# A fused attention and MoE kernel: single token tiles at the start of the first layer, a held weight load, and paired fifth tiles

## The chip, the core and the metric

The kernel runs on one core of one Trainium2 chip. The metric is the device time of one execution in microseconds; the median of the runs is what counts. PE is the matmul engine, PEld its weight loads, DVE the vector engine, ACT the scalar engine, POOL the engine that issues the weight transfers, and SP the queue that issues most other transfers. Each engine works through its own instructions in a fixed order.

## The reference: linear attention, then two matrix products with a gate between them

For 8 batches, 8 heads, 576 tokens and a head size of 64 the reference computes

```
phi(x)  = concat(relu(x) * cos(pos), relu(x) * sin(pos))     # 64 -> 128
kv      = phi(k)^T v          z = sum over tokens of phi(k)  # per batch and head
attn    = phi(q) kv / (phi(q) z + 1e-6)
x       = attn, heads side by side                           # 4608 tokens x 512
h       = x @ w_in                                           # 512 -> 2048
out     = (h * cos(h)) @ w_out                               # 2048 -> 512
```

The inputs q, k, v, w_in and w_out and the output are float32.

## The kernel before

**Tiles.** The 576 tokens of a batch lie on 128 partitions: even and odd partitions hold two blocks of 64 rows. One block has five tokens for each partition and the other four, so a batch has four full token tiles of 128 and a fifth tile in which only 64 rows, every other one, are its own. Which block has the five alternates with the batch. The fifth tiles of two batches fill one tile of 128 tokens, so there are nine groups of 512 tokens for the two layers: `c` = 0 to 7 are the four full tiles of batch `c`, and `c` = 8 collects the fifth tiles of all batches (`xR`).

**Attention of a batch.** `load` (L332) issues the transfers of q, k and v on SP, two for each (four and five tokens for each partition). `prep` (L355) makes relu times cos or sin of one token tile on ACT or DVE, `cast_v` (L369) casts v, and `kv` (L383) multiplies: 40 matmuls of 65 columns, the 65th being a column of ones that gives z. Its result is copied to `kvz`. `q_pe` (L414) transposes a q tile with 8 matmuls and a copy; later batches use a transposing transfer instead (`q_dma`). `num` (L435) multiplies a q tile with `kvz`, 8 matmuls of 65 columns; DVE and ACT then make `den`, `rec` and `x`; `x_pe` (L489) transposes x into `xT`, and `x_dma` does it with a transfer.

**Fifth tiles before.** Each batch has its own prep and transpose of its fifth q tile, into `qT4[b % 2]`. With an odd batch, `num` multiplies both, `parts` of two matmuls accumulating in one bank: the rows that are not a batch's own are zeros there. For that, `first_attention` clears the fifth place of the raw q, k and v on DVE (L962), and cs has zeros in those rows. For batch 0 the fifth q tile is prepared in `late_q0` (L1039), behind the first gate of layer 1, and the one of batches 0 and 1 goes through `num` in `second_attention` (L987).

**Layer 1 and layer 2.** `layer1` (L522) of the first two groups goes by quarters of w_in; each step is 8 matmuls of 256 columns (two token tiles, two blocks of 128 of the 2048 columns) into one of three banks `M1`, followed by `gate` (L511): ACT makes the cosine (as a sine) into `ch`, and DVE multiplies. `layer2_plain` (L771) does layer 2 of group 0 with 512 columns in the two banks `M2`. Later groups use products of sums of blocks (seven products in place of eight), for which `w_in_sums` (L615) writes sums of weights into tiles `WS0` to `WS2`.

**The start.** PE runs filler matmuls (`warm`, L913) until q has landed. POOL issues the weight transfers in `weights` (L920): a small copy waits until k has landed, then come all four quarters of w_in, then w_out's first two quarters behind a copy that waits for w_in's first. `hold_raw` (L945) holds the transfers of batch 1 on a small copy that reads w_in's first quarter.

**Order.** All steps are added to a `Plan` (L142) with their reads and writes. A table of numbers at the top, `KEYS` (L17), one for each step, gives the place of each step in the order, and for steps that can go to several engines which engine does it. Every engine's queue is that order, so it is written out once for the whole kernel.

Of the kernel before, what the change touches and what calls it, by code (L numbers as in the profile page):

```python
# [12 lines left out]
F32 = mybir.dt.float32  # L13
# [180 lines left out]
def kernel(  # L194
# [9 lines left out]
    nc = tc.nc  # L204
# [127 lines left out]
    def load(b, nm, due, hs=(slice(0, H),)):  # L332
        m, n = raw[nm], b % 2
        for h in hs:
# [3 lines left out]
            def go5(h=h, five=five):  # L338
                nc.sync.dma_start(out=blocks(m, n)[:, h], in_=five)
# [711 lines left out]
    for c in range(2, NC):  # L1051
        if c < B:
            attention(c)
# [40 lines left out]
```

## Time and profile before

| what | value |
|---|---|
| median of 3 runs | 281.59 us (280.68 to 282.78) |
| the profiled execution, its own time | 280.85 us |
| its span, first to last instruction | 279.0 us |
| PE busy, PEld, DVE, ACT | 269.2, 217.3, 251.4, 218.9 us |
| mean granted TensorE clock | 0.999 |
| read from HBM, written to it | 36.74 MB, 9.44 MB |
| transposing transfers qT<-KQ after 59 us, time from issue to landing | 29, median 5.1 us |
| matmuls of `num` (L450) | 320 |

The lines of the trace name an engine, a line of the kernel, an operation, and what it writes and reads. Times in the timeline are from the start of the span. A group's mean is the duration of one instruction, and matmuls overlap, so the distance between the starts of two matmuls is shorter than the duration: 16 matmuls of `num` with a mean of 193 ns each take 0.48 us. `MEMSET`, `COPY` and `CAST` are DVE's or POOL's; `LDWEIGHTS` is a weight load of 128 by 128, one ahead of each matmul.

### The profile page before, as it was taken

The numbers are of one execution on the slowest core, as the hardware profiler recorded it, in microseconds if no ns is written. First come the engines' busy times: TensorE is split into PE (matmuls) and PEld (weight loads), VectorE is DVE, ScalarE is ACT, GpSimd is POOL, SyncE is SP. The second block draws the span as 40 slices with busy tenths as digits, with TensorE's granted clock in tenths as the row PEclk, the third lists the DMA queues.
The fourth block names the chain that finished last, engine by engine and source line by source line (L and its number), as shares of the span: only waits on it lengthen the run. The fifth ranks groups of instructions, "written<-read, shape, count | busy, mean of one in ns | idle before, by whom it ended". The sixth has DMA issues, their size and how long they took to land.

```text
span 279.0 us, 6853 instructions
## 1 busy us (share of the span) xinstructions
PE 269.2 (96%) x2715; PEld 217.3 (78%) x2715; DVE 251.4 (90%) x449; ACT 218.9 (78%) x401; POOL 8.3 (3%) x21
## 2 busy tenths in 40 slices
PE   7779999999999999999999999999999999999994
PEld 2458767678766677789879887998788888888883
DVE  2977798999999999999999999999999999998872
ACT  2856698899999999999999999984684686777210
POOL 1430020000000000000000000000000000000000
PEclk9999999999999999999999999999999999999999
DMA  6999999999999999999999999737210400200324
GB/s 208 315 201 232 281 312 282 309 218 172 328 269 253 210 288 247 310 235 230 245 264 195 346 277 265 154 58 205 39 39 4 188 2 0 78 0 2 151 78 150
DMA packets 77599, 53.30 MB, mean 191 GB/s; under 512 B 46080, under 2 KB 75264, under 8 KB 77568
## 3 DMA queue, kind: packets, MB, share of 16 engines
q1 hardware_dynamic: 72608, 48.12, 67.7%
q0 software_dynamic: 4224, 4.19, 9.3%
q10 hardware_dynamic: 736, 0.57, 0.6%
q8 instruction: 21, 0.34, 0.5%
q14 instruction: 10, 0.08, 0.1%
HBM read 36.74 MB, written 9.44 MB: 166 GB/s over the span
## 4 chain that ended last, share of the span: by engine, by line
PE 85%; DMA 5%; ACT 4%; DVE 3%; issue 2%; ACTq 0%
PE M L849 33%; PE M L685 15%; PE M L542 8%; PE M L582 7%; PE TR L685 6%; PE M L784 4%; PE ATT L450 3%; DMA qT<-KQ 3%; PE ATT L391 3%; DMA qm<-in_q_dram 2%; ACT KQ L364 2%; PE TR L582 1%; ACT ch L514 1%; PE M L420 1%; DVE KQ L365 1%
## 5 line engine op out<-in xcount | busy, mean ns | idle before, releaser
L514 ACT ACTIVATE ch<-M 128x512 f32<-128x512 f32 x90 | 53.9, 603 | 14.0 <-PE M L685 6.8
L849 PEld LDWEIGHTS <-gT 128*128 128x128 f16 x560 | 54.1, 98 | 8.2
L519 DVE TENSOR_TENSOR gT<-M,ch 128x512 f16<-128x512 f32 x84 | 55.9, 685 | 4.5 <-ACT ch L514 4.0
L849 PE MATMUL M<-w_out_sb,gT 128*128 128x256 f16 x448 | 56.4, 273 | 0.0
L364 ACT ACTIVATE KQ<-km,CS 128x512 f16<-128x512 f32 x56 | 38.9, 732 | 0.5 <-DMA km<-in_k_dram 0.5
L364 ACT ACTIVATE KQ<-qm,CS 128x512 f16<-128x512 f32 x48 | 33.5, 728 | 4.4 <-DMA qm<-in_q_dram 4.2
L685 PEld LDWEIGHTS <-w_in_sb 128*128 128x128 f16 x320 | 31.0, 98 | 4.6 <-issue 0.2
L849 PE MATMUL M<-T,S 128*128 128x256 f16 x256 | 31.5, 273 | 0.0
L318 ACT ACTIVATE ost<-M 128x512 f32<-128x512 f32 x32 | 19.2, 600 | 15.0 <-PE M L849 9.5
L542 PE MATMUL M<-xT,w_in_sb 128*128 128x256 f16 x256 | 30.1, 272 | 0.6 <-DVE gT L519 0.5
L542 PEld LDWEIGHTS <-w_in_sb 128*128 128x128 f16 x256 | 24.6, 98 | 4.8 <-issue 1.2
L582 PE MATMUL M<-xT,w_in_sb 128*128 128x512 f16 x112 | 27.9, 379 | 0.0
L849 PEld LDWEIGHTS <-S 128*128 128x128 f16 x256 | 24.9, 98 | 3.4
L476 DVE TENSOR_TENSOR x<-ATT,rec 128x512 f16<-128x512 f32 x32 | 22.1, 692 | 2.5
L685 PEld LDWEIGHTS <-WS 128*128 128x128 f16 x216 | 20.6, 98 | 2.6
L582 PEld LDWEIGHTS <-w_in_sb 128*128 128x128 f16 x128 | 11.9, 98 | 9.2
L365 DVE TENSOR_SCALAR KQ<-qm,CS 128x512 f16<-128x512 f32 x32 | 14.2, 479 | 4.8 <-DMA qm<-in_q_dram 4.8
L450 PEld LDWEIGHTS <-qT 128*128 128x128 f16 x320 | 14.7, 98 | 4.4 <-issue 1.4
L323 DVE TENSOR_TENSOR S<-gT 128x2048 f16<-128x2048 f16 (+1 forms) x16 | 17.2, 1083 | 0.0
L450 PE MATMUL ATT<-kvz,qT 128*128 128x65 f16 x288 | 15.3, 194 | 0.9 <-DVE kvz L406 0.4
L323 DVE TENSOR_TENSOR gT<-Z,ch 128x1024 f16<-128x1024 f32 x13 | 15.9, 1219 | 0.3
L698 DVE TENSOR_TENSOR Z<-M,Z 128x512 f32<-128x512 f32 x22 | 14.9, 686 | 0.9 <-PE M L685 0.5
(138 smaller groups left out, 448.6 us busy)
## 6 DMA issues: line engine op xcount, KB each, us to landing
out_dram<-ost SPq DMA_DIRECT2D x33, 256.0 KB, 2.7
qm<-in_q_dram SPq DMA_DIRECT2D x8, 640.0 KB, 5.7
km<-in_k_dram SPq DMA_DIRECT2D x8, 640.0 KB, 6.5
qm<-in_q_dram SPq DMA_DIRECT2D x8, 512.0 KB, 6.0
km<-in_k_dram SPq DMA_DIRECT2D x8, 512.0 KB, 6.5
vm<-in_v_dram SPq DMA_DIRECT2D x6, 640.0 KB, 6.8
vm<-in_v_dram SPq DMA_DIRECT2D x6, 512.0 KB, 6.6
w_in_sb<-in_moe_w_in_dram POOLq DMA_DIRECT2D x4, 512.0 KB, 8.6
```

The source lines that it names most:

```text
L318: "ACT": lambda: nc.scalar.activation(out=out_, in_=in_, func=AF.Copy),
L323: return lambda: q.tensor_tensor(out=out_, in0=in0, in1=in1, op=op)
L364: fn = {"ACT": lambda: nc.scalar.activation(out=out_, in_=in_, func=AF.Relu, scale=sc), "DVE": lambda: nc.vector.tensor_scalar(out=out_, i ...
L365: "DVE": lambda: nc.vector.tensor_scalar(out=out_, in0=in_, scalar1=0.0, scalar2=sc, op0=ALU.max, op1=ALU.mult)}
L450: nc.tensor.matmul(bank[hb][:, hh * D1:(hh + 1) * D1], lhsT=a[:, h, :], rhs=z[:, h, :], start=(i == 0), stop=(i == len(parts) - 1))
L476: nc.vector.tensor_tensor(out=split(x16[n][:, hs, :], k), in0=A[:, :, :, 0:D], in1=split(rec[n][:, hs], k).unsqueeze(3).broadcast_to((P, k ...
L514: act(0.5, due, lambda: nc.scalar.activation(out=ch[c], in_=bank, func=AF.Sin, bias=math.pi / 2.0, scale=1.0), [key], [("ch", c)])
L519: dve(0.61, due, lambda: nc.vector.tensor_tensor(out=dst, in0=a, in1=b, op=ALU.mult), [key, ("ch", c), *rd], dkeys)
L542: nc.tensor.matmul(M1[m][:, jj * 2 * P:(jj + 1) * 2 * P], lhsT=w_in_sb[:, cc, j * P:(j + 1) * P], rhs=X[:, cc, ts], start=(jj == 0 and cc ...
L582: nc.tensor.matmul(M, lhsT=w_in_sb[:, cc, j * P:(j + 1) * P], rhs=X[:, cc, :], start=(cc == 0), stop=(cc == NCT - 1))
L685: nc.tensor.matmul(bank[0][:, j * TH:(j + 1) * TH], lhsT=a(cc, j), rhs=b[:, cc, :], start=(first and j == 0 and cc == 0), stop=(last and j ...
L849: nc.tensor.matmul(bank[0][:, tt * MH:(tt + 1) * MH], lhsT=a[:, j, tt * P:(tt + 1) * P], rhs=b[:, j, :], start=(first and (apart or tt == ...
```

## The change

Three things change, and with them the whole table `KEYS`, so that the order and the engines of many other steps differ too (1,407 steps before, 1,396 after).

*First layer of batch 0.* Quarter 0 of w_in is done by `first_tile`: one token tile at a time, 16 matmuls of 128 columns into one bank. Quarters 1 to 3 stay at 256 columns. The banks of this layer are six, the three `M1`, `TR` and the two `M2`, in place of three. In PE's order the four single tiles stand like this: tile 0, the transposes of x of tiles 3 and 2, then a second tile, a third, one step of 256 columns, and the last tile.

*w_in's second half.* `weights` issues two quarters; `more_weights` issues the other two behind a copy that reads the last V cast of batch 0, and then w_out as before. In POOL's order the hold for q of batch 1 and then the one for k now stand behind w_out's first and second quarter.

*Fifth tiles of q.* The fifth place of the raw q is filled by both batches of a pair, each in its own rows, and is prepared and transposed once, with the odd batch, into one tile `qT4`. Only `num` separates them: for each head two matmuls with 64 weight columns each, every second column of `qT4`, one for the even batch and one for the odd, into rows 0 to 63 and 64 to 127 of the bank. cs gets a sixth column with the fifth tile's factors for all rows. The fifth rows of `xR` are then the even batch's 64 followed by the odd one's, and the stores of group 8 read neighbouring rows. For batches 0 and 1, q is loaded without its fifth token, q's memset is gone, and `first_fifth_tile` loads, prepares and multiplies the fifth tokens later, in the part of group 2; their `kvz` are kept until then in the tile `WS2`, whose weight sums therefore come behind that `num`. `late_q0` is gone.

```diff
     def load(b, nm, due, hs=(slice(0, H),)):
...
-                nc.sync.dma_start(out=blocks(m, n)[:, h], in_=five)
+                nc.sync.dma_start(out=blocks(m, n)[:, h, 0:n5, :], in_=five[:, :, 0:n5, :])
...
+            n5 = NT if b < 2 and nm == "q" else NT + 1
...
+    def load_q5(b, due):
+        five = tokens(src["q"][b])[0]
+        pl.add("SP", 0.65, 0, due, lambda: nc.sync.dma_start(
+            out=blocks(Q5, b), in_=five[:, :, NT, :]),
+            [], [("q5", b), ("Z3", 0, 0)], dma=(R * H * D * 4 / 1e3, 150.0, 55), late=0.9, lazy=LAZY)
...
     def num(b, t, due, pair=None):
...
-        parts = [(qdst(b, t)[0], kvz[b % 2])]
...
-            parts.insert(0, (qT4[1 - b % 2], kvz[1 - b % 2]))
...
-                for i, (a, z) in enumerate(parts):
+                for n2 in range(2) if t == NT else [None]:
+                    rows_, cols, z = (slice(0, P), slice(0, P), kvb(b)[0]) if n2 is None else (
+                        slice(n2 * R, (n2 + 1) * R), slice(n2, P, 2), kvb(b - 1 + n2)[0])
                     nc.tensor.matmul(
-                        bank[hb][:, hh * D1:(hh + 1) * D1], lhsT=a[:, h, :], rhs=z[:, h, :],
-                        start=(i == 0), stop=(i == len(parts) - 1))
+                        bank[hb][rows_, hh * D1:(hh + 1) * D1], lhsT=a[:, h, cols], rhs=z[:, h, :],
+                        start=True, stop=True)
...
+    def first_tile(X, xk, G, t):
+        ring = BANKS + BANKS2
+        M, mk = ring[m1n[0] % len(ring)]
+        m1n[0] += 1
+        due = start[0] + t * width[0] / NJT
+        ts = slice(t * P, (t + 1) * P)
+
+        def mm():
+            for j in range(4):
+                for cc in range(NCT):
+                    nc.tensor.matmul(
+                        M[:, j * P:(j + 1) * P], lhsT=w_in_sb[:, cc, j * P:(j + 1) * P], rhs=X[:, cc, ts],
+                        start=(j == 0 and cc == 0), stop=(j == 3 and cc == NCT - 1),
+                        skip_group_check=True)
+        full[mk] = True
+        pe(4 * NCT, MMT, due, mm, xk[t:t + 1] + [("w_in", 0)], [mk])
+        gate(M, mk, G[:, 0:4, ts], [("g", 0, j, t) for j in range(4)], due + 1.5)
...
     def layer1(c):
...
-            for quarter in range(4):
+            if c == 0:
+                for t in range(NT):
+                    first_tile(X, xk, G, t)
+            for quarter in range(1 - min(c, 1), 4):
...
-                        m = m1n[0] % NM1
+                        ring = BANKS + BANKS2 if c == 0 else BANKS[0:NM1]
+                        M, mk = ring[m1n[0] % len(ring)]
...
     def weights():
...
-        for g in range(4):
+        w_in_load(0, 2)
...
+    def more_weights():
+        def hold():
+            nc.gpsimd.tensor_copy(
+                out=w_in_sb[0:1, 0, Dff // 2:].rearrange("p (g f) -> p g f", g=2)[:, :, 0],
+                in_=V1[0:1, NT, HB, 0:1].broadcast_to((1, 2)))
+        pl.add("POOL", 0.2, 0.3, 0, hold, [("V1", NT, HB)], [("w_in", g) for g in range(2, 4)])
+        w_in_load(2, 4)
...
     def first_attention():
-        for i, nm in enumerate("qkv"):
+        for i, nm in enumerate("kv"):
...
+    def first_fifth_tile(due):
+        for n in range(2):
+            load_q5(n, due)
+        for g in range(2):
+            prep(1, "q", NT, g, "", due + 4)
+        q_pe(1, NT, TR, ("TR", 0), "ACT", due + 5)
+        n = num(1, NT, due + 7)
+        x_pe(1, NT, n, TR, ("TR", 0), "ACT", due + 8)
...
-    def late_q0():
-        for g in range(2):
-            prep(0, "q", NT, g, "DVE", 24, after=[("g", 0, 0, 0)])
-        q_pe(0, NT, TR, ("TR", 0), "ACT", 25)
```

More of the change, by code (lines that the diff above doesn't have):

```diff
@@ L254 @@
     qT = [sb(f"qT{t}", [P, H, P]) for t in range(NT)]
-    qT4 = [sb(f"qT4_{n}", [P, H, P]) for n in range(2)]
+    qT4 = sb("qT4", [P, H, P])
     kvz = [sb(f"kvz{n}", [P, H, D1]) for n in range(2)]
@@ L400, in kv @@
                + [("V1", t, h) for t in range(NT + 1) for h in hs], [keys[hb]])
-        Z = kvz[b % 2].rearrange("p (b h) d -> p b (h d)", b=2)
-        zk = [("kvz", b % 2, i) for i in range(2)]
+        Z = kvb(b)[0].rearrange("p (b h) d -> p b (h d)", b=2)
+        zk = [("kvz", kvb(b)[1], i) for i in range(2)]
         if pair:
@@ L622, in tt @@
             sums(due, CH2 * GW, ws[n], a, b, op, [("w_in", g // 2), ("w_in", 2 + g // 2)] + rd,
[L623 removed]
+                 wr + [("WS", n, g)] + q + ([("kvz", 2 + i, j) for i in range(2) for j in range(2)] if g == 2 else []),
+                 lazy=20.0)
         tt(3, a11, a21, ALU.subtract, [("a21", g)], [])
@@ L934, in hold2 @@
                 in_=w_in_sb[0:1, 0, 0:1].broadcast_to((1, 4)))
-        if W_FIRST is None:
-            pl.add("POOL", 0.2, 0.3, 0, hold2, [("w_in", 0)], [("w_out", g) for g in range(4)])
-            w_out_load(0, 2)
+        pl.add("POOL", 0.2, 0.3, 0, hold2, [("w_in", 0)], [("w_out", g) for g in range(4)])
+        w_out_load(0, 2)
     def w_out_load(g0, g1):
@@ L998, in second_attention @@
                 prep(1, "k", t, g, "", T + 1)
-        for t in range(NT + 1):
+        for t in range(NT):
             due = T + 2 + t + 6 * (t > 1)
@@ L1022, in attention @@
         kv(b, T + 8)
-        for t in range(NT + 1):
+        for t in range(NT + b % 2):
             due = T + 8 + 1.2 * t
```

56 lines of the change are left out of this document (34 added, 22 removed), and 241 rows, old and new, of the table KEYS.

## The prediction, made before the changed kernel ran

> **What bounds the kernel now.** Read in this order: the page's busy sums, busy time by stage (windows), the chain of waits, the timeline of 7 to 43 us, the DMA view. First the page's sums:
>
> ```profile
> PE 269.2 (96%) x2715; PEld 217.3 (78%) x2715; DVE 251.4 (90%) x449; ACT 218.9 (78%) x401; POOL 8.3 (3%) x21
> ```
>
> Then the stages (stretch, its length, busy time of each engine, granted clock, DMA share, GB/s):
>
> ```profile
> 12.00:22.00 10.00, 8.25 (x114) 5.53 (x113) 7.97 (x24) 5.95 (x15) 4.62 (x11) 1.00 1.17 201
> 22.00:43.00 21.00, 20.28 (x176) 15.51 (x174) 17.38 (x37) 16.90 (x32) 1.66 (x3) 1.00 1.16 274
> 43.00:60.00 17.00, 17.00 (x208) 12.34 (x205) 15.75 (x35) 14.75 (x33) 0.00 (x0) 1.00 0.92 282
> 60.00:110.00 50.00, 49.56 (x535) 37.42 (x534) 47.93 (x89) 48.53 (x94) 0.00 (x0) 1.00 1.14 251
> 110.00:180.00 70.00, 69.93 (x727) 58.60 (x725) 68.45 (x118) 69.19 (x128) 0.00 (x0) 1.00 1.10 255
> 180.00:274.00 94.00, 94.00 (x909) 82.81 (x908) 87.14 (x136) 57.28 (x98) 0.00 (x0) 1.00 0.21 66
> ```
>
> After 22 us PE is idle for 0.72 + 0 + 0.44 + 0.07 + 0 = 1.23 us in all, at full clock, and it then works almost to the end. So a change can win only by giving PE less to do, by starting its dense work earlier, or out of those 1.23 us. ACT and DVE are nearly full from 60 to 180 us, but PE does not wait for them there: work taken from them gains nothing by itself. What a matmul costs when PE is dense is in the chain of waits (start, length, what):
>
> ```profile
> 44.22 0.89 PE M L420 x16
> 61.25 0.87 PE M L542 x8
> 62.12 1.21 PE ATT L391 x40
> 145.54 0.48 PE ATT L450 x16
> ```
>
> These are 56 ns for 128 moving columns, 109 for 256, and 30 for 65. Now the start, from the timeline (start, duration, engine, line; in brackets the idle time before it and what ended it):
>
> ```profile
> 9.33 0.69 DVE L319 COPY qT<-M 128x1024 f16<-128x1024 f16 x1
> 10.24 0.69 DVE L319 COPY qT<-M 128x1024 f16<-128x1024 f16 x1 [0.22 <-PE M L420]
> 10.62 1.95 ACT L364 ACTIVATE KQ<-km,CS 128x512 f16<-128x512 f32 x3 [0.46 <-DMA km<-in_k_dram]
> 14.59 0.88 DVE L379 CAST V<-vm 128x256 f16<-128x256 f32 x4
> 16.91 0.29 PE L450 MATMUL ATT<-kvz,qT 128*128 128x65 f16 x4 [0.36 <-DVE kvz L406]
> 21.02 0.76 DVE L476 TENSOR_TENSOR x<-M,rec 128x256 f16<-128x256 f32 x2
> 21.96 5.47 PE L542 MATMUL M<-xT,w_in_sb 128*128 128x256 f16 x48
> 31.28 5.40 PE L542 MATMUL M<-xT,w_in_sb 128*128 128x256 f16 x48 [0.54 <-DVE gT L519]
> 32.61 0.76 SPq L339 DMA_DIRECT2D vm<-in_v_dram  x1
> 42.84 1.37 PE L391 MATMUL ATT<-V,KQ 128*128 128x65 f16 x40
> ```
>
> Dense work starts at 21.96, when the last x of batch 0 is there. At 31.28 PE waited for a bank. At 42.84 comes kv of batch 1, whose last V was cast only at 42.6, since its transfer, issued at 32.61, landed 8.4 us later, at 41.0 (DMA view, one issue):
>
> ```profile
> vm<-in_v_dram SPq DMA_DIRECT2D x1, 320.0 KB, 8.4
> ```
>
> The DMA share is 1.16 from 22 to 43 us: the transfers run without a break, so their bytes set this landing.
>
> **The change part by part.** Removed PE work, from the instruction order of both kernels: 8 transposes of L420, 8 x 56 = -0.45 us. Layer 1 of batch 0, quarter 0: 32 x 109 = 3.49 becomes 64 x 56 = 3.58, +0.09. The fifth tiles keep their 64 matmuls of 65 columns, but each now has 64 weight columns, taken with a stride of two, and writes one half of the rows. No row has such weights. From below: two halves side by side, 15 each, 64 x (15-30) = -1.0. Next row: 56 (L420), 64 x 26 = +1.7. From above: each runs alone, with its whole duration of 193 ns (group of L450), 64 x 163 = +10.4. I take 30, the row of the same operation, line and moving size: 0.
>
> Removed elsewhere: eight q preps (0.73 ACT or 0.48 DVE each), one q copy, a 0.48 us memset, three transposing DMAs on SP (1.8 us each), offset by 2 transfers of 131 KB on SP (0.65 us of issue each). Summing every instruction at its group's mean, ACT falls by 1.9 us and DVE by 3.5. PE covers all of it: 0. The moved fifth tile of batches 0/1 and the weight sums that now wait for it (4 x 0.42 DVE) go into 60 to 110 us, where DVE idles 2.1 and ACT 1.5 us; without that cover they would cost 1.7. But counted to the 48th gate, the work ahead of it falls by 3.4 (ACT) and 2.7 us (DVE), so that stretch gets no fuller. The SP transfers and loads behind the two new issues are prefetches: 0; 1.3 us if not.
>
> w_in quarters 2 and 3 wait for the last V cast, about 14.3, and are issued near 15 and 16 instead of 12.9 and 13.7. Quarter 1 lands only at 19.3 in the same queue, and quarter 2 (22.7) is not read before about 28: 0, and even 2 us later it is covered. On POOL they pass ahead of the w_out hold, which waits to 17.06 anyway; the hold for k of batch 1 goes behind one more issue, about 0.6 us. The busy DMA engines cover it; uncovered, it is 0.6.
>
> The start. q of batch 0 loads 131 KB less. k's and q's last landings (10.5 and 7.2) are 1.18 MB apart, 353 GB/s, so all three arrive 0.37 earlier: q 6.8, k 10.15, v 13.35. DVE no longer copies q first (9.33, 10.24): from 10.28 it has 5 preps of 0.45 and 8 casts of 0.22, to 14.3; ACT 5 of 0.65 and 2 of 0.36, to 14.25; before, the last cast ended at 15.47. Then kv to 15.2, one q copy each and kvz to 15.65, and the first num ends its wait at 15.7 instead of 16.91. The chain of den, rec, x is the same from there (x 0 ends 17.45 instead of 18.44, x 3 at 20.5 instead of 21.78), so dense work begins near 20.95: -1.0. The single tile ahead of it (16 x 56 = 0.90) replaces 8 x 109 = 0.87, since tile 1 stands behind x 3's transposes on PE: starting by tiles gains nothing itself. Six banks remove the bank waits, 0.7.
>
> Then the bytes bind. PE would reach kv of batch 1 at 42.84 - 1.0 - 0.7 + 0.1 = 41.2, but v lands 262 KB earlier at best, 0.73 us at 360 GB/s: 40.3, and four or five casts of 0.36 follow. Bounds for kv: -0.3 (landing unmoved, casts slower) and -1.6 (PE decides). I take -0.9, near the landing. Behind it PE has 8 transposes fewer: -0.45 (the late q0 is gone ahead of it, a third q transpose moves ahead of it, and one paired transpose replaces two behind it).
>
> Later waits: the new order has other waits for transposes. Before, three of 0.2 to 0.4 (1.0 in all, L450); I add 0.3, bounds -0.5 and +1. Stores from 64 neighbouring rows instead of every other: same bytes, 0, bounds 0.5 either way.
>
> Sum: -0.9 - 0.45 + 0 + 0.3 = -1.05. The profiled execution took 280.85 (span 279.0 and 1.85 around it): 279.8. The median of the runs, 281.59, is 0.74 above it: **280.5**.
>
> **Rivals.**
> *The halves cost 56 ns.* Strided, half-wide weights load at a rate that a 30 ns matmul cannot hide: +1.7 gives 282.2. For it: PEld is already busy 78% and L450 spaces 29 to 35 ns, with nothing left over; against: no row shows a width deciding. [...]
>
> *The transfers take back the start.* k goes 0.6 later and kv of batch 1 stays at 42.84: 0 - 0.45 + 0.3 = about 281.4.
>
> *Faster.* v lands early enough, PE decides at kv (-1.6), halves run side by side (-1.0), and no new waits: -1.6 - 0.45 - 1.0 = 278.5.
>
> *Slower: the halves run one after another.* If the array empties between the two row halves, each costs its duration: +10.4, 291; at the 98 ns of a weight load's row, +4.3, 284.8. It decides from 30 + (2.8 + 1.05)/64 = 90 ns on. Against it: matmuls of different lines follow each other without a gap in this trace.
>
> **How the numbers follow.** Forecast 0.43 (its own range 279.0 to 281.8), halves at 56 ns 0.23, transfers 0.12, faster 0.10, slower 0.12. A measurement here tells about 1%, 2.8 us, from no change: faster 0.10, same 0.43 + 0.23 + 0.12 = 0.78, slower 0.12. The range leaves the last two out: from the forecast's low end, 279.0, to halves at 56 ns with no gain at kv, 281.4 + 1.7 = 283.1, rounded to 283.3.
>
> **What would show it.** Last V cast of batch 0 near 14.3; first 256-column group after the tiles at 21 to 22; no bank wait from 22 to 36; kv of batch 1 near 41.9 with PE idle before it; fifth tiles at 30 ns a matmul, 16 in 0.5 us; PE idle after 43 us still under 1.5. Wrong if the halves' spacing is far above 56, if v of batch 1 lands after 41, or if PE waits for ACT or DVE from 60 to 180 us.

## The result, and the profile after

The changed kernel is slower by a little: a median of 283.37 us (282.31 to 283.99, 16 runs) against 281.75 (280.09 to 283.45, 16 runs), a ratio of 1.0056 with an interval of 1.0031 to 1.0080. In a later set of runs, `r1`, it took 283.32 against 280.48 (1.0086, 1.0058 to 1.0114). The profiled execution took 282.31 us, with a span of 280.5 and a clock of 0.997; it is the fastest of the 16, as the one before (280.85, span 279.0) lies 0.9 under its own median. What is to be explained is thus 1.5 us of span. (`e13` and `e15` below each had one run in a slower state, left out of their medians.)

The page's sums of the changed kernel:

```profile
PE 269.6 (96%) x2739; PEld 216.5 (77%) x2739; DVE 247.0 (88%) x443; ACT 217.6 (78%) x397; POOL 8.4 (3%) x22
```

DVE and ACT have 4.4 and 1.3 us less to do, and PE is busy 0.4 us more. That is not more work: matmuls overlap, and ahead of a wait a matmul's whole duration (273 ns for 256 columns, at a spacing of 109) counts as busy. The stages (stretch, its length, busy time of PE, PEld, DVE, ACT and POOL, clock, DMA share, GB/s):

```profile
12.00:22.00 10.00, 9.51 (x145) 7.19 (x144) 7.77 (x26) 6.73 (x15) 4.53 (x11) 1.00 1.19 201
22.00:43.00 21.00, 20.05 (x206) 15.51 (x204) 16.03 (x32) 15.47 (x31) 1.66 (x3) 1.00 1.14 265
43.00:60.00 17.00, 16.80 (x162) 11.68 (x159) 16.26 (x38) 13.31 (x26) 0.00 (x0) 1.00 0.99 298
60.00:110.00 50.00, 48.99 (x554) 36.52 (x553) 48.21 (x90) 49.04 (x96) 0.00 (x0) 1.00 1.11 256
110.00:180.00 70.00, 69.86 (x719) 57.87 (x720) 68.08 (x116) 67.99 (x124) 0.00 (x0) 1.00 1.00 239
```

PE is busier by 1.26 us from 12 to 22, and less busy by 0.23, 0.20, 0.57 and 0.07 in the four stretches behind. Busy times hide part of a wait, so I also made a ledger from the starts of the matmuls: each costs about 216, 109, 56 or 31 ns (for 512, 256, 128 or 65 columns), and what lies beyond that before the next start is idle. (With exactly these costs, work comes out 0.6 us lower and idle time 0.6 us higher in both kernels; the differences stay within 0.02.)

| us | before | after | difference |
|---|---|---|---|
| PE's work | 264.24 | 263.88 | -0.36 |
| idle from the first matmul to 40 us | 7.40 | 5.19 | -2.21 |
| idle 40 to 60 | 0.26 | 2.01 | +1.75 |
| idle 60 to 274 | 1.46 | 2.42 | +0.96 |
| last matmul's end (1.59 and the above) | 274.95 | 275.09 | +0.14 |
| from there to the end of the span | 4.05 | 5.40 | +1.35 |
| span | 279.0 | 280.5 | +1.5 |

So in these two executions the start gains what was meant, 2.2 us. PE loses 1.75 of it around 41 us and 0.96 later, and the last 1.35 are lost with PE already done. The waits of the changed kernel behind 60 us come back in the profile of `r1` within 0.01 us each; those of the kernel before differ between executions, so the 0.96 is less sure than the 1.35 (see `e2` and `e10` in the table of runs). The places, in PE's timeline (start, duration, line, tiles, count; in brackets the idle time before and its releaser):

```profile
19.40 1.05 PE L544 MATMUL M<-xT,w_in_sb 128*128 128x128 f16 x16
20.74 1.06 PE L544 MATMUL M<-xT,w_in_sb 128*128 128x128 f16 x16
...
40.39 0.61 PE L431 MATMUL M<-IDENT,KQ 128*128 128x128 f16 x8 [0.66 <-DVE KQ L373]
41.29 0.62 PE L431 MATMUL M<-IDENT,KQ 128*128 128x128 f16 x8 [0.30 <-DVE KQ L373]
41.75 1.64 PE L402 MATMUL ATT<-V,KQ 128*128 128x65 f16 x40
...
67.61 0.42 PE L462 MATMUL ATT<-kvz,qT 128*128 128x65 f16 x8 [0.30 <-DVE x L488]
...
69.42 0.41 PE L462 MATMUL ATT<-kvz,qT 128*128 128x65 f16 x8 [0.27 <-DVE x L488]
```

From 20.74 on the tiles follow each other without a wait. At 40 us three transposes of q and kv of batch 1 stand in a row with no group of layer 2 between them. Before, eight matmuls of 512 columns, 1.9 us, stood just ahead of kv:

```profile
41.12 1.89 PE L784 MATMUL M<-w_out_sb,gT 128*128 128x512 f16 x8
```

The end, from the DMA view of the last 11 us (GB/s in 40 slices; then the issues, KB each, us from issue to landing), first before, then after:

```profile
GB/s 0 0 0 0 0 0 0 0 0 0 0 0 7 365 380 365 387 372 30 290 335 309 134 246 142 235 216 0 0 0 0 0 0 0 0 0 0 0 0 0
out_dram<-ost ACTq DMA_DIRECT2D x1, 256.0 KB, 3.2
out_dram<-ost ACTq DMA_DIRECT2D x1, 128.0 KB, 2.5
```

```profile
GB/s 0 0 0 0 0 0 0 0 0 0 0 0 0 0 0 60 216 201 201 156 164 291 313 264 246 291 324 309 298 242 171 67 0 0 0 0 0 0 0 0
out_dram<-ost ACTq DMA_DIRECT2D x1, 256.0 KB, 4.5
out_dram<-ost ACTq DMA_DIRECT2D x1, 128.0 KB, 4.1
```

The bytes are the same. Before, the first slices run at 365 to 387 GB/s; after, at 156 to 216, and the stores of 256 and 128 KB take 0.8 to 1.7 us longer from issue to landing.

### The profile page after: what moved, and what is told of

It reads as the page before. It is cut to its first block, busy times and chain, and to the rows that moved or that the text cites. A ratio compares the mean times of both kernels' runs of the same rounds, so it can differ in the third digit from the quotient of the medians.

```text
span 280.5 us, 6911 instructions
## 1 busy us (share of the span) xinstructions
PE 269.6 (96%) x2739; PEld 216.5 (77%) x2739; DVE 247.0 (88%) x443; ACT 217.6 (78%) x397; POOL 8.4 (3%) x22
## 4 chain that ended last, share of the span: by engine, by line
PE 82%; DVE 8%; ACT 4%; DMA 3%; issue 1%; SPq 1%; DVEq 0%; ACTq 0%
PE M L888 34%; PE M L724 16%; PE M L616 9%; PE TR L724 6%; PE M L576 4%; PE M L823 3%; PE ATT L462 3%; DMA km<-in_k_dram 3%; DVE gT L531 2%; PE ATT L402 2%; DVE KQ L373 2%; PE TR L616 1%; DVE x L488 1%; ACT KQ L372 1%; PE M L544 1%
## 5 line engine op out<-in xcount | busy, mean ns | idle before, releaser
L526 ACT ACTIVATE ch<-M 128x512 f32<-128x512 f32 x87 | 50.4, 602 | 12.9 <-PE M L576 6.0
L531 DVE TENSOR_TENSOR gT<-M,ch 128x512 f16<-128x512 f32 x81 | 54.1, 683 | 6.6 <-ACT ch L526 6.1
L724 PEld LDWEIGHTS <-w_in_sb 128*128 128x128 f16 x320 | 30.9, 98 | 4.4 <-issue 0.2
L888 PE MATMUL M<-T,S 128*128 128x256 f16 x256 | 32.4, 273 | 0.0
L318 ACT ACTIVATE ost<-M 128x512 f32<-128x512 f32 x30 | 17.9, 600 | 15.7 <-PE M L888 10.6
L372 ACT ACTIVATE KQ<-qm,CS 128x512 f16<-128x512 f32 x36 | 25.3, 733 | 4.0 <-DMA qm<-in_q_dram 4.0
L576 PE MATMUL M<-xT,w_in_sb 128*128 128x256 f16 x208 | 25.2, 273 | 0.0
L576 PEld LDWEIGHTS <-w_in_sb 128*128 128x128 f16 x224 | 21.3, 98 | 3.1 <-DVE gT L531 0.3
L724 PEld LDWEIGHTS <-WS 128*128 128x128 f16 x216 | 20.7, 98 | 2.6
L373 DVE TENSOR_SCALAR KQ<-qm,CS 128x512 f16<-128x512 f32 x34 | 15.2, 484 | 5.3 <-DMA qm<-in_q_dram 5.2
L616 PEld LDWEIGHTS <-w_in_sb 128*128 128x128 f16 x128 | 12.0, 98 | 9.3
L462 PEld LDWEIGHTS <-qT 128*128 128x128 f16 (+1 forms) x320 | 13.5, 100 | 6.7 <-issue 3.5
L746 ACT ACTIVATE ch<-Z 128x1024 f32<-128x1024 f32 x14 | 14.9, 1062 | 1.0 <-DVE Z L737 0.9
```

What stands on the lines that cost most here:

```text
L318: "ACT": lambda: nc.scalar.activation(out=out_, in_=in_, func=AF.Copy),
L372: fn = {"ACT": lambda: nc.scalar.activation(out=out_, in_=in_, func=AF.Relu, scale=sc), "DVE": lambda: nc.vector.tensor_scalar(out=out_, i ...
L373: "DVE": lambda: nc.vector.tensor_scalar(out=out_, in0=in_, scalar1=0.0, scalar2=sc, op0=ALU.max, op1=ALU.mult)}
L462: nc.tensor.matmul(bank[hb][rows_, hh * D1:(hh + 1) * D1], lhsT=a[:, h, cols], rhs=z[:, h, :], start=True, stop=True)
L526: act(0.5, due, lambda: nc.scalar.activation(out=ch[c], in_=bank, func=AF.Sin, bias=math.pi / 2.0, scale=1.0), [key], [("ch", c)])
L531: dve(0.61, due, lambda: nc.vector.tensor_tensor(out=dst, in0=a, in1=b, op=ALU.mult), [key, ("ch", c), *rd], dkeys)
```

## The experiments

Three theories, one for each loss. **T1**: a store that reads 64 neighbouring rows moves at half the rate of one that reads every other row; rival: the later landing comes from the new order of the issues. **T2**: around 41 us PE waits since transfers (their bytes) make v or the casts late; rivals: T2b, batch 1's k preps fill DVE and ACT; T2c, the q chain itself, of preps, transposes and copies, is what PE waits for. **T3**: at 67 to 71 us too little layer work stands between a `num` and the next one, so PE waits for the chain of den, rec and x; rival: the engines are simply full there, and an order that removes the wait moves it. The ratios are against the kernel before, run beside each on the same chip (they need not be exactly the quotient of the two medians); idle times are the ledger's, from one profile each. In the last column 1.59 and 1.21 differ by a single wait of 0.37 us that the changed kernel has at 110 us (110.0 in its own profile, 111.6 in `r1`): it falls inside the column in some runs and behind it in others.

| run | us | before | ratio (95%) | idle 40-60 | idle 60-110 |
|---|---|---|---|---|---|
| e1 | 281.53 | 280.27 | 1.0038 (1.0021-1.0055) | 2.39 | 1.21 |
| e2 (before + rows) | 280.77 | 280.27 | 1.0024 (1.0007-1.0041) | 0.02 | 1.62 |
| e3 | 284.01 | 280.27 | 1.0125 (1.0100-1.0150) | 2.02 | 1.22 |
| e4 | 284.57 | 280.27 | 1.0155 (1.0125-1.0186) | 2.00 | 2.81 |
| r1 | 283.32 | 280.48 | 1.0086 (1.0058-1.0114) | 2.78 | 1.21 |
| e5 | 296.73 | 280.48 | 1.0564 (1.0521-1.0608) | 2.01 | 1.22 |
| e6 | 283.89 | 280.48 | 1.0112 (1.0067-1.0158) | 2.01 | 2.02 |
| e7 | 282.52 | 280.48 | 1.0072 (1.0046-1.0097) | 1.56 | 1.59 |
| e8 | 282.75 | 280.11 | 1.0113 (1.0078-1.0147) | 2.01 | 1.22 |
| e9 | 282.39 | 280.11 | 1.0078 (1.0059-1.0096) | 2.01 | 1.59 |
| e10 (before + less k) | 280.92 | 280.11 | 1.0024 (0.9999-1.0048) | 0.13 | 0.20 |
| e11 | 283.53 | 280.11 | 1.0109 (1.0083-1.0135) | 2.01 | 1.21 |
| e12 | 282.26 | 280.67 | 1.0069 (1.0042-1.0096) | 1.75 | 1.21 |
| e13 | 286.77 | 280.67 | 1.0192 (1.0153-1.0230) | 0.10 | 1.22 |
| e14 | 282.57 | 280.67 | 1.0054 (1.0029-1.0078) | 2.00 | 1.59 |
| e15 | 285.22 | 280.67 | 1.0178 (1.0142-1.0214) | 0.09 | 0.77 |
| e16 | 283.87 | 280.61 | 1.0110 (1.0085-1.0135) | 3.12 | 1.54 |
| e17 | 283.17 | 280.61 | 1.0095 (1.0066-1.0125) | 2.40 | 1.60 |

### The stores: e1, e2, e14 and e5

e1 lets the changed kernel's stores of group 8 read every other row again; e2 lets the kernel before read neighbouring ones.

```diff
-            put(due, dst..., O[n * R:(n + 1) * R, i0:, f],
+            put(due, dst..., blocks(O, n)[:, i0:, f],
...
-            put(due, dst..., ost[o][n * R:(n + 1) * R, i, 0:MH],
+            put(due, dst..., blocks(ost[o], n)[:, i, 0:MH],
```

> The changed kernel with one thing undone: the last group's stores (the fifth tiles) read every other row of the output tile again instead of 64 neighbouring rows. The rows of the fifth tiles so go to the wrong places of the output; every instruction and all bytes are the same. Theory 1 (the stores from neighbouring rows cost the end of the span): the stretch from the last matmul's end to the span's end falls from 5.4 us to about 4.05 us, the 256 KB stores land 2.5 to 3.2 us after issue instead of 3.3 to 4.5, the 128 KB ones in 2.2 to 2.5 instead of 3.9 to 4.1, and the time is about 1.35 us below the changed kernel's 283.4, so near 282.0, within 0.3 us of the kernel before. Rival (the stores are slow since they are issued later or closer together, or the layout costs nothing as the prediction had it): the tail stays at 5.4 us and the time within 0.4 us of 283.4.

> The kernel before with that one thing done: the last group's stores read 64 neighbouring rows instead of every other row; the rows of the fifth tiles so go to the wrong places of the output. Theory 1: the last matmul ends where it did (274.95 us), the tail grows from 4.05 us to about 5.4 us, and the time rises by about 1.35 us, a ratio near 1.005. Rival: tail 4.05 us, ratio 1.000 within 0.001.

The DMA view of e1, the same 11 us (its last stores are issued 1.8 us later than the changed kernel's; the first five slices are an earlier store):

```profile
GB/s 417 357 432 417 134 0 0 0 0 0 0 0 0 0 0 0 0 0 0 0 0 0 290 410 380 387 365 328 343 346 321 194 235 216 0 0 0 0 0 0
out_dram<-ost ACTq DMA_DIRECT2D x1, 256.0 KB, 3.2
out_dram<-ost ACTq DMA_DIRECT2D x1, 128.0 KB, 2.8
```

From the first 256 KB store's issue to the last landing e1 takes 4.94 us and the changed kernel 6.25; its span ends 4.1 us after the last matmul, not 5.4. In e2 it takes 6.12 instead of 5.53, and 4.6 us instead of 4.05 after the last matmul. So the rows alone cost 0.6 us in the old order of issues and 1.3 us in the new one, and the new order alone costs under 0.1 (e1 against the kernel before). That e2 loses less fits its 128 KB stores being issued 1.69 us behind the 256 KB ones, against 1.09 in the changed kernel; no run tests that reason. The two issues shown above take 4.3 and 3.6 us in e2, with nothing but the rows changed.

The packets in the traces show the cost itself. The two 256 KB stores, one from rows 0 to 63 and one from rows 64 to 127, are issued within 0.01 us, yet the second one's packets start only as the first one's end (from 275.70 on, the first one's ending at 275.90, in the changed kernel; 274.25 and 274.41 in the kernel before). A packet of 2 KB of the first store takes 162 ns in the median in the changed kernel and in e2, and 86 ns in the kernel before, e1 and e14: 1.6 us for its 128 packets in the changed kernel, 0.8 in the kernel before.

e14 keeps the right rows: before layer 1 of group 8 four copies on POOL put the fifth rows back into alternating columns, and the stores read every other row.

```diff
+        if c == B:
+            X = flat(raw["v"])[:, 4 * SM:8 * SM].rearrange("p (c s) -> p c s", c=NCT)
+            for i in range(NT):
+                ts = slice(i * P, (i + 1) * P)
+                pl.add("POOL", 0.9, 0, start[c] - 8, lambda ts=ts: nc.gpsimd.tensor_copy(
+                    out=X[:, :, ts].rearrange("p c (r n) -> p c r n", n=2),
+                    in_=xR[:, :, ts].rearrange("p c (n r) -> p c r n", n=2)),
+                    [("xR", i), "AL"], [("xRp", i)])
```

> The changed kernel with the last group's stores from every other row again and the right output: POOL, which is idle, puts the columns of the four tiles of the last group's x into alternate order in another buffer (four copies of 128x512) ahead of layer 1, so that the matmuls read contiguous columns (strided reads by the matmuls took 242 ns instead of 109). Theory 1: the stretch from the first 256 KB store of the end to the last landing falls from 6.25 to 4.95 us, matmuls of the last group stay 109 ns apart, and the time falls by 1.3 us, to a ratio near 1.004. Rival: the copies on POOL delay the last group by their own time (about 1 us for its last tile) and the time stays within 0.4 us of the changed kernel.

The DMA view of e14, the same 11 us:

```profile
GB/s 104 0 0 0 0 0 0 0 0 0 0 0 0 0 0 0 0 0 365 387 365 365 384 339 339 332 339 179 220 201 0 0 0 0 0 0 0 0 0 0
out_dram<-ost ACTq DMA_DIRECT2D x1, 256.0 KB, 3.2
out_dram<-ost ACTq DMA_DIRECT2D x1, 128.0 KB, 2.9
```

The rate is back at 365 to 387 GB/s, first issue to last landing is 4.95 us, and the span ends 4.1 us after the last matmul. PE's idle time from 180 to 274 us is 0.54 us longer there, 0.41 of it a wait for a gate on DVE at 227.1, so this way of mending gives part of the gain back. In the medians, `r1` and e1, the same kernel but for the rows, ran 12 times each on one chip: 1.0086 against 1.0038, the intervals just apart, a difference of 1.35 us. Two more pairs, apart by e14's edit alone, ran on one chip: e15 against e13 (-1.55 us in the median) and e17 against e16 (-0.7); their intervals overlap, so they bear T1 out in sign. T1 is shown: e1 has the changed kernel's order of issues and the old landing, so the rival falls.

e5 had meant to do the same without copies, by letting layer 1 of group 8 read its columns in alternating order.

```diff
+        def cols(ap):
+            return ap if c < B else ap.rearrange("p (t n r) -> p t r n", t=2, n=2)
...
-   bank[0][:, j * TH:(j + 1) * TH], lhsT=a(cc, j), rhs=b[:, cc, :],
+   bank[0][:, j * TH:(j + 1) * TH], lhsT=a(cc, j), rhs=cols(b[:, cc, :]),
```

> The changed kernel with the last group's stores from every other row, and its output right: layer 1 of the last group reads its token columns in the interleaved order (64 tokens of one batch and 64 of the other by turns) as its moving operand, so that the rows of the output tile alternate again. Theory 1: the time from the issue of the first 256 KB store of the end to the last landing falls from 6.25 us to 4.9 us and the time by about 1.3 us against the changed kernel in this call (ratio to before about 0.0045 lower), if the strided reads of the moving operand cost nothing; they would show as 256-column matmuls of that group spaced more than 109 ns. Rival (the rows do not matter in the median): within 0.4 us of the changed kernel.

It lost 16.25 us against its own before. The same group in e5 and in the changed kernel:

```profile
234.50 1.13 PE L720 MATMUL M<-xR,w_in_sb 128*128 128x256 f16 x4
```

```profile
233.42 0.60 PE L724 MATMUL M<-xR,w_in_sb 128*128 128x256 f16 x4
```

The starts of these matmuls are 241 to 245 ns apart instead of 109: 112 of them, 15.0 us. So the rows can be mended by a copy on the idle POOL, and not by the reading of PE.

### Around 41 us: e3, e7, e8, e9, e10, e11, e12

e3 and e11 put quarter 0 of w_in ahead of quarter 1 in POOL's queue (the changed `KEYS` issue quarter 1 first, and 3 before 2). In e11 the hold for w_out also reads quarter 1, so that what is behind it keeps its time.

```diff
-KEYS: steps 12, 13 at 11630, 10730; steps 52, 53 at 15160, 14260   # 52, 53 in e3 alone
+KEYS: steps 12, 13 at 10730, 11630; steps 52, 53 at 14260, 15160
...
-                in_=w_in_sb[0:1, 0, 0:1].broadcast_to((1, 4)))          # e11
+                in_=w_in_sb[0:1, 0, Dff // 4:Dff // 4 + 1].broadcast_to((1, 4)))
```

> The changed kernel with the order of the transfers of w_in put right: quarter 0 issued ahead of quarter 1, and quarter 2 ahead of quarter 3 (in the changed kernel they are issued 1, 0 and 3, 2). Expected of both theories: quarter 0 lands near 16.5 to 17 us instead of 19.3, the hold that waits for it ends near 17 instead of 19.3, and batch 1's k is issued near 19.2 instead of 21.6. Theory 2 (the bytes bind: what is issued earlier only waits in the queues): v of batch 1 still lands 40 to 40.6 us, kv of batch 1 stays within 0.5 us of 41.75 and the time within 0.5 us of 283.4. Rival (the late issue has held batch 1 back): v lands 1 to 2 us earlier, PE's 2.0 us of idle time at 40 to 44 us go, and the time falls by 1 to 2 us.

> The changed kernel with quarter 0 of w_in issued ahead of quarter 1 and the hold that releases w_out and batch 1's k waiting for quarter 1, so that everything behind it is issued when it is in the changed kernel, and only the single token tiles find quarter 0 2 to 3 us earlier (PE waited 0.3 to 1.5 us for it at 19 to 20.6 us, by the profile). If what PE gains at its start is lost at 40 to 44 us (theory 2b), the wait before the first single token tile goes, the idle time at 40 to 44 us grows by as much, and the time stays within 0.4 us of the changed kernel (ratio 1.007 to 1.010). Rival (the start's gain does reach the end): 0.5 to 1.2 us faster than it, a ratio of 1.004 to 1.007.

In e3 quarter 0 landed at 17.2 instead of 19.3, k of batch 1 was issued at 19.5, and PE then waited for w_out:

```profile
35.74 5.34 PE L816 MATMUL M<-w_out_sb,gT 128*128 128x512 f16 x24 [1.61 <-DMA w_out_sb<-in_moe_w_out_dram]
```

w_out's second quarter came at 35.6 instead of 33.0, v of batch 1 as before at 40.66. e11 has no such wait, and its idle time of 40 to 60 us is unmoved, 2.01. In the profiled execution the order of the quarters, which the prediction had not seen, costs nothing: in e3 the first tile begins at 19.47, with quarter 0 there since 17.2, and in the changed kernel at 19.40, with quarter 0 there since 19.3. In other executions it does cost: of the 13 profiles with this start, three had quarter 0 only at 20.1 to 20.7 (`r1`, e1 and e16), and PE waited 1.2 to 1.5 us for it.

> The changed kernel as it is, beside the runs of this call, so that they can be compared with it. Expected: a ratio to the kernel before between 1.003 and 1.010, since the same kernel with alternate store rows measured 1.0038 and the two profiles give the neighbouring rows 1.3 us of 281 (0.0046): near 1.008 if that cost stands in the median as in the profiles (theory 1), near 1.004 if it does not.

The first tile in `r1`:

```profile
20.28 1.05 PE L544 MATMUL M<-xT,w_in_sb 128*128 128x128 f16 x16 [1.01 <-DMA w_in_sb<-in_moe_w_in_dram]
```

The holds for w_out and for batch 1 read quarter 0 too, so all that is behind them came later: v of batch 1 landed at 42.0, kv of batch 1 began at 43.36, later than the 42.84 of the kernel before, and the last matmul ended 1.6 us later than in the changed kernel's own profile. So such executions lose the start's gain altogether. How many of the runs are of that kind, and so what share of the medians' 1.6 us it has, is not known; e3 and e11, which put quarter 0 first, were not faster.

e7 loads one of the four row blocks of w_out's second quarter, e8 prepares one head of eight of batch 1's k, e9 does both, and e10 is e8's edit in the kernel before.

```diff
+        nc.gpsimd.memset(w_out_sb[:, 5:8, :], 0.001)                          # e7, e9
...
-            js = slice(g * NJT // 4, (g + 1) * NJT // 4)
+            js = slice(g * NJT // 4, (g + 1) * NJT // 4 - 3 * (g == 1))
...
+        if nm == "k" and b == 1:                                              # e8, e9, e10
+            out_, in_ = out_[:, 0:1], in_[:, 0:1]
```

> The changed kernel with three quarters of one quarter of w_out not loaded (three of its four blocks of 128 rows hold a constant, written by POOL at the start); that leaves out about 390 of the 512 KB that this transfer writes. Theory 2 (from 14 to 41 us the transfers' bytes bind, all DMA engines being busy, and so PE's 2.0 us of idle time at 40 to 44 us give back what the start gained): at the 206 GB/s of the weight transfers this is 1.9 us of transfer time, v of batch 1 lands 1.3 to 2 us earlier than 40.3 to 41.4, kv of batch 1 begins near 40 to 40.5 us instead of 41.75, and the time falls by 1 to 1.9 us against the changed kernel. Rival (preparing q and v on VectorE and ScalarE, or PE's order, sets kv of batch 1): v lands earlier and kv of batch 1 moves by less than 0.5 us, the time by less than 0.5 us.

> The changed kernel, in which the ten instructions that prepare batch 1's k (six on VectorE, four on ScalarE, between 34.5 and 42 us) do one head of eight, the rest of the tile keeping batch 0's values; order, transfers and waits stay. Theory 2b (formed since the shorter transfer of w_out brought v 1.9 us earlier and left PE's idle time at 40 to 44 us: VectorE and ScalarE, both busy without a gap from 34.5 us, when k has landed, to 44 us, set kv of batch 1): about 1.8 us of work goes from each engine, PE's idle time at 40 to 44 us falls from 2.0 to 2.8 us to about 1 us (then v, landing at 40.6 us, binds), and the time falls by about 1 us against the changed kernel, to a ratio near 1.005. Rival 2a (transfers): no change, a ratio of 1.0086 within 0.001.

> Both at once: batch 1's k prepared for one head of eight, and three quarters of one quarter of w_out not loaded, so that v lands near 38.7 us. Theory 2b: with the vector work gone v's landing is the next bound, and with that gone too PE's idle time at 40 to 44 us falls under 0.5 us; the time falls by about 2 us against the changed kernel, to a ratio near 1.001. Rival (PE's own order keeps the idle time there, or hands the gain back at 67 to 71 us): idle time at 40 to 44 us stays over 1 us, or it goes and the waits at 67 to 71 us grow by as much, with a ratio over 1.004.

> The control: the kernel before with batch 1's k prepared for one head of eight. There PE is later and has 0.28 us of idle time at 40 to 50 us, so theory 2b expects at most 0.3 us, a ratio of 0.999 to 1.000. If it gains 1 us or more here too, the vector work binds whatever PE does, and it says nothing on where the changed kernel's gain went.

What PE waited for from 39 to 45 us (total, times, longest), in the changed kernel, in e7 and in e9:

```profile
PE M L431 <- DVE KQ L373: 1.0, 2, 0.7
PE M L431 <- ACT qT L318: 0.2, 1, 0.2
```

```profile
PE M L431 <- DVE KQ L373: 0.6, 2, 0.3
PE ATT L402 <- ACT V L386: 0.2, 1, 0.2
PE M L431 <- ACT qT L318: 0.2, 1, 0.2
```

```profile
PE M L433 <- ACT qT L318: 0.9, 2, 0.7
PE ATT L404 <- ACT V L388: 0.2, 1, 0.2
```

In e7 the last v of batch 1 landed at 38.66 instead of 40.58, and kv began at 41.50 instead of 41.75: T2 falls, since 1.9 us of transfers bought 0.25. (Its idle time is 1.56 from 40 to 60 and 0.43 just ahead, 1.99 together.) In e8 it stayed. In e9 the waits for DVE are gone and as much waiting for ACT's copy of qT stands in their place, idle 2.01 again. T2b falls. e10 finds no gain in the kernel before either. ACT's queue in e9 shows why (a copy that waits for PE, six casts, a copy):

```profile
39.83 1.02 ACT L318 ACTIVATE qT<-M 128x1024 f16<-128x1024 f16 x1 [0.94 <-PE M L433]
40.75 1.94 ACT L388 ACTIVATE V<-vm 128x256 f16<-128x256 f32 x6
42.59 1.01 ACT L318 ACTIVATE qT<-M 128x1024 f16<-128x1024 f16 x1
```

e12 takes the other side away: the copies of batch 1's first two q tiles do one head of eight.

```diff
-        copies(due, {"ACT": 0.95, "DVE": 0.69}, dst, ps, [key], [dkey], ...)
+        one = slice(0, 1 if b == 1 and t < 2 else H)
+        copies(due, {"ACT": 0.95, "DVE": 0.69}, dst[:, one], ps[:, one], [key], [dkey], ...)
```

> The changed kernel, in which the two ScalarE copies of batch 1's transposed q (tiles 0 and 1, 1.02 us each) copy one head of eight, the rest keeping batch 0's values. Theory 2c (formed since transfers and the preparation of k, taken away together, left TensorE's idle time at 40 to 44 us at 2.0 us: ScalarE works off a chain there in its own order, copy of q 1.02 us, six casts of v 1.94 us, copy of q 1.01 us, copy of kv 0.60 us, each behind or ahead of TensorE's steps, and no group of layer matmuls stands between): about 0.8 us comes off each copy, the idle time at 40 to 44 us falls from 2.0 us to about 1 us, unless v's landing near 40.6 us holds the casts, then to about 1.4 us. Whether it reaches the end is another question: what PE gains there can be lost at 67 to 71 us, where its order leaves too little cover; ratio 1.005 to 1.0086. Rival (the chain is not ScalarE's): idle time stays at 2.0 us.

PE's waits of 39 to 45 us in e12:

```profile
PE M L431 <- ACT qT L318: 0.5, 1, 0.5
PE M L431 <- DVE KQ L373: 0.3, 1, 0.3
PE TR L463 <- ACT WS L318: 0.2, 1, 0.2
```

Idle 40 to 60 goes from 2.01 to 1.75 alone. So two chains of about equal length end at kv, DVE's preps and gates, and ACT's copy, casts and copy; taking either leaves the other. That fits T2c. Both were not taken away together, so T2c is what is left, not what is shown. What the profile does show is that PE has nothing else there: the next group of layer 2 needs a bank whose copy stands in DVE's queue behind the preps, at 43.16.

```profile
42.55 0.68 DVE L531 TENSOR_TENSOR gT<-TR,ch 128x512 f16<-128x512 f32 x1
43.16 0.68 DVE L319 COPY ost<-M 128x512 f32<-128x512 f32 x1
```

### 67 to 76 us, and the order as a whole: e4, e6, e13, e15, e16, e17

Two groups of layer 2 (steps 363 and 364) and one of layer 1 (280) are moved between the `num`s of batch 2.

```diff
-KEYS: steps 363, 364, 280 at 71020, 74820, 72620
+KEYS: steps 363, 364, 280 at 68820, 70800, 70540   # e4
+KEYS: steps 363, 364, 280 at 68820, 70540, 72380   # e6
```

> The changed kernel with three groups of matmuls moved in TensorE's order at 68 to 73 us, so that two of them instead of one stand between the attention products of batch 2's successive token tiles; no other change. Theory 3 (the chain product, denominators, reciprocal and product with x on the one pair of banks takes 1.8 us and one group of 0.87 us does not cover it): the three waits of 0.46, 0.44 and 0.40 us at 67.4, 69.2 and 70.9 us fall to under 0.3 us in sum, the last matmul ends 0.8 to 1.1 us earlier than 275.1, and the time falls by about 1.0 us. Rival (PE only waits elsewhere, since another engine or transfer sets the pace between 60 and 110 us): the waits reappear before 110 us and the time stays within 0.4 us of 283.4.

> The second try at the order of 67 to 73 us in the changed kernel; the first brought one group of layer 1 so early that it waited 0.96 us for its bank, and lost more than it gained. Here a layer 2 group stands behind the layer 1 group between the second and the third token tile of batch 2, another between the third and the fourth, and the layer 1 group that the first try moved stays behind them. Theory 3: the waits of 0.46 and 0.44 us at 67.4 and 69.2 us go (under 0.1 us each), that of 0.40 us at 70.9 us may stay, no new wait over 0.3 us appears before 110 us, and the time falls by about 0.9 us against the changed kernel. Rival: the waits only move, the time stays within 0.3 us.

PE's waits from 66 to 76 us in the changed kernel, then in e6:

```profile
PE ATT L462 <- DVE x L488: 0.6, 2, 0.3
PE TR L508 <- DVE x L488: 0.2, 1, 0.2
```

```profile
PE TR L424 <- ACT xT L311: 0.8, 1, 0.8
PE M L609 <- DVE gT L524: 0.5, 1, 0.5
PE TR L501 <- DVE x L481: 0.2, 1, 0.2
```

The waits for x at the two `num`s are gone, as T3 says: with two groups (1.75 us) between them the chain of 1.8 us is covered, with one (0.87) it is not. But more came back a few us later, for a copy on ACT and a gate on DVE: idle 60 to 110 rose to 2.02, where runs whose wait at 110 us falls outside this column, as it does here, have 1.21 (e4: 2.81, part of it a bank that I moved into the way). The rival holds for the sum.

In e13 the whole order of 12 to 160 us was changed, in e16 that of 35 to 80 us with the transfers' queues left as they are; e15 and e17 add e14's edit.

```diff
-KEYS = (
-    0, 660, 0, 0, 650, 1300, 1950, 2600, 3250, 3900, 4550, 10230, 11630, 10730, 8501, 7522,
...
+KEYS = (                                                                   # e13
+    10, 50, 20, 30, 40, 60, 70, 80, 90, 100, 110, 350, 460, 390, 121, 132, 140, 492, 152, 161, 170,
...
```

> The changed kernel with the same instructions, in another order on TensorE, VectorE, ScalarE between about 12 and 160 us (a few of them on another engine), chosen so that TensorE has a group of layer matmuls ready wherever the changed kernel's profile shows it waiting at 40 to 44 and 67 to 71 us. Stores and transfers stay. Theory 2c and 3 (the start's gain was given back to the order of the instructions): the idle time at 40 to 44 us falls under 0.8 us and that at 67 to 71 us under 0.4 us, the last matmul ends 1.5 to 2 us earlier than in the changed kernel, and the time falls by as much, to a ratio near 1.002. Rival (data or an engine's work binds there, and waits only move): the idle time before 115 us stays within 0.6 us of what it was, ratio over 1.006.

> Both: the new order and the stores by way of POOL, output right. If the theories hold and the two gains add (1.3 us at the end, 1.5 to 2 us before it), 3 us under the changed kernel: a ratio to the kernel before of 0.996 to 0.999. If the gains do not add, 1.002 or more.

> The changed kernel with the instructions of TensorE, VectorE and ScalarE between about 35 and 80 us in another order (some 40 of them on VectorE instead of ScalarE or the other way), all transfers issued in the order they had. Theories 2c and 3: TensorE's idle time at 40 to 48 us falls from 2.0 to 2.8 us to under 1.8 us, that at 67 to 71 us from 1.3 us to under 0.3 us, no new wait over 0.4 us before 160 us, and the time falls by 1.2 to 1.7 us against the changed kernel, to a ratio of 1.002 to 1.005. Rival (something binds there that order does not change): ratio over 1.007.

> The same order and the last group's stores from every other row by way of POOL, output right. If both theories hold and their gains add, the time lies 1.2 to 1.7 us under the kernel with the stores by way of POOL alone (ratio 1.0054), a ratio of 0.999 to 1.002: all that the changed kernel lost is then found. If not, 1.004 or more.

e13 has no wait left at 41 and 67 us (idle 40 to 60: 0.10), and is the slowest but e5, since k of batch 1 is issued ahead of w_out's second quarter there:

```profile
36.19 1.02 PE L795 MATMUL M<-w_out_sb,gT 128*128 128x512 f16 x4 [1.91 <-DMA w_out_sb<-in_moe_w_out_dram]
```

and PE waited another 1.54 at 146.8. With that wait ahead of it, kv of batch 1 began at 44.01, 2.3 us later than in the changed kernel, so its 0.10 does not show that the new order covers the wait at 41 us. In e16, which keeps the transfers, a gate on DVE takes the place of the preps: PE waits 1.2 us for it at 42.7, and idle 40 to 60 is 3.12. (Part of e16's loss is the late quarter 0 that `r1` has too.) e4 and e6 removed the waits at the `num`s that they were made for, e13 and e16 those at 67 to 71 us, and each got others as long or longer. Whether some order keeps the lead of the start stays open. No version here beats the kernel before; with the right rows e14 comes nearest (1.0054).

## Why the prediction was wrong

It forecast 1.05 us less by the profiled execution, and the spans say 1.5 more: 2.55 to account for. Its terms:

| term | forecast (bounds) | measured |
|---|---|---|
| start, banks, kv of batch 1 | -0.9 (-1.6 to -0.3) | -0.46, idle to 60 us |
| transposes and quarter 0 | -0.45 (and +0.09 left out) | -0.36 |
| halves | 0 (-1.0 to +10.4) | about 0, in the idle rows |
| later waits | +0.3 (-0.5 to +1) | +0.96, idle 60 to 274 |
| stores of group 8 | 0 (-0.5 to +0.5) | +1.35 |

**The step that failed** is "Stores from 64 neighbouring rows instead of every other: same bytes, 0, bounds 0.5 either way". It measured +1.35, 1.35 of the 2.55, and is the one term outside its bounds. Its reason counted bytes, when the same bytes from other partitions moved at 156 to 216 GB/s in the first slices instead of 365 to 387 (the kernel before and e14; e1 has 365 to 410 there), with the old landing restored by the rows alone (e1). In the old order of issues the rows cost 0.6 us (e2), just over the bound. Every rival had put its loss on PE or the loads; none had looked behind the last matmul, where nothing covers a transfer, and no row of the kernel before shows a store from neighbouring rows. In the first slices, where one store moves at a time, the rate is about half, and a packet of the first store takes 162 ns instead of 86; what sets it, no run shows.

**The start was right, its account at kv was not.** The tiles begin without a bank wait, the last V cast of batch 0 ended by 14.5 (14.3 forecast), the first group of 256 columns came at 22.52 (21 to 22), and kv of batch 1 at 41.75 (41.9). But that kv came early was no gain by itself: eight matmuls that stood ahead of it before now stand behind it, and PE idled 2.0 us instead. "Then the bytes bind" is refuted (e7): v landed at 40.58, before 41, and 1.9 us earlier still kv moved by 0.25. The term was half the size forecast, within its bounds. It also rested on quarter 0 of w_in coming first, as before; issued second, it made the tiles wait 1.2 us in `r1`, which the prediction had no term for.

**The later waits** were put at +0.3 and measured +0.96, just inside, against one profile of the kernel before; e2 and e10, which have its order (e10 with less work on k), idled 1.62 and 0.20 us from 60 to 110 us, so a part of it can be chance. "From 60 to 180 us PE does not wait" for the full DVE and ACT no longer held: 0.87 us of layer work between two `num`s is less than the chain's 1.8. That PE's idle time after 43 us would stay under 1.5 held by the windows (0.20 + 1.01 + 0.14 = 1.35), which is a poor test: the ledger has 2.42 after 60 us alone.

**The halves** were right at 0, for another reason than the row taken. Four matmuls of 512 columns (0.86 us from 74.52, so to 75.38), then sixteen halves:

```profile
74.52 1.03 PE L616 MATMUL M<-xT,w_in_sb 128*128 128x512 f16 x4
75.47 0.45 PE L462 MATMUL ATT<-WS,qT 128*64 128x65 f16 x16
75.86 1.05 PE L576 MATMUL M<-xT,w_in_sb 128*128 128x256 f16 x8
```

From 75.38 to 75.86 are 0.48 us, as the sixteen took before. Within, the two halves of a head start 3 ns apart and the heads 31 ns, 0.25 us in all; some 95 ns are lost on entering and as much on leaving. So the rival of 56 ns a matmul did not come: the sixteen loads of 64 weight columns, 111 ns each and overlapping, took 0.34 us together. The rivals on the transfers and on "faster" did not come either: kv did not stay at 42.84, and later waits did come. The slower rival had the right sign by a wrong mechanism.

## What to carry to other kernels

Cost a transfer by the partitions it touches as well as by its bytes, above all the last stores, which nothing covers: here stores from 64 neighbouring rows each ended 1.3 us later than stores from every other row, 0.6 us in the old order of issues. A gain at the start is kept only if PE has other work wherever it now arrives early (here 1.75 of 2.2 us went again around 41 us); ask of each early arrival what chain (not what transfer) ends last there, and what stands in PE's order meanwhile. Where two chains end together, shortening one of them shows little (idle time of 2.01 us stayed 2.01 in e9 and became 1.75 in e12), and moving the wait is not removing it (e6).

## What the runs showed of the hardware

- A 256-column moving operand read in alternating order of two stretches of 64 columns: starts 241 to 245 ns apart instead of 109 (e5).
- POOL interleaves three 128x512 tiles of f16 in 1.88 us together and a fourth in 0.76 us (e14).
- Stores of 1.05 MB from 64 neighbouring rows a piece take 6.25 us from first issue to last landing, from every other row 4.94 (changed kernel and e1). A packet of 2 KB of the first store takes 162 ns instead of 86 (changed kernel and kernel before), and two 256 KB stores issued within 0.01 us move one after the other, whichever rows they read: the second one's packets start 0.16 us before the first one's last ends in the kernel before, 0.21 us in the changed kernel.
- Two matmuls with 64 weight columns each, into the two halves of a bank's rows, start 3 ns apart (1 to 5) and the next pair 31 ns later; a group of sixteen costs about 95 ns at either end (changed kernel, at 75.47).
